# Grouping the logits, softmax and accumulation of the first 20 token tiles in twos

## The chip, the cores and the metric

The kernel runs on one core of one Trainium2 chip. The metric is device time in microseconds (us), the median of repeated executions. One further execution was profiled; all rows below are from it.

## The reference, cut to what matters

Three stages follow one another: attention whose mask lets a query see the keys of its own cluster, a feed-forward layer with the activation h * cos(h), and a soft mixture of experts whose dispatch weights are a softmax over all 3072 tokens. The change touches the second stage and the start of the third.

```
x = attention output, 3072 tokens x 512
h = x @ w_in                                  # 3072 x 2048
g = h * np.cos(h)
x = g @ w_out                                 # 3072 x 512
logits = x @ phi                              # 3072 x 32 slots
d = np.exp(logits - logits.max(0)); d /= d.sum(0) + 1e-09     # over tokens
slot_input = d.T @ x                          # 32 x 512
slot_out = per expert: relu(slot_input @ w1) @ w2
c = np.exp(logits - logits.max(1)); c /= c.sum(1) + 1e-09     # over slots
out = c @ slot_out
```

## The kernel before, in words

Attention takes the first half of the time. Then comes the loop of the feed-forward layer, called the MLP here: 24 tiles of 128 tokens, each in four chunks of 512 hidden columns, so 96 chunks numbered c. For chunk c TensorE computes h (`hchunk`, 12 matmuls of 512 columns into one of three PSUM buffers, `h`). ScalarE and VectorE turn it into g = h * cos(h): a scaled copy on ScalarE and two passes on VectorE (`post1`), then sine, square and a last pass on VectorE that writes `gg` and is the last reader of the PSUM buffer (`post2`; the square is on ScalarE for even chunks and on VectorE for odd ones). TensorE transposes g (`gtr`, tile `gt`), ScalarE copies the transposed chunk to SBUF (`gev`, tile `gts`), and TensorE multiplies it with w_out @ phi, folded beforehand, into the logits of the tile (`logit`, tile `lp`). The product with w_out itself is not formed per token: the kernel accumulates d.T @ g and multiplies that by w_out at the end.

When the four chunks of a tile are through, a running softmax follows over some iterations: `soft1` copies the logits (`lps`), `soft2` sums them up with a constant matrix in both orientations (`lf`, `lt`) and takes the maxima on VectorE (`mrun`, `ng`, `rn`), `softx` and `softe` take the exponentials on ScalarE (`d`, `corr`, `e`), `soft3` updates the sums and writes the normalised weights `ck`, `soft3b` transposes `d` (`dt`, copied to `dts`), `soft4` multiplies it with the tile's g (`accp`) and `soft5` adds that to `acc`. Sine and exponential are in different tables of ScalarE, so each of these softmax steps has two table loads around it.

All instructions stand in the order in which the code writes them, engine by engine; nothing is reordered, and an engine waits at the head of its queue. The loop over c is the order: in iteration c stand `hchunk(c)`, `post2(c-2)`, `post1(c-1)`, `gev(c-4)` and `gtr(c-3)`. So `hchunk(c)` reuses the PSUM buffer that chunk c-3 left, and waits for the `gg` pass of chunk c-3. The softmax steps hang on the last chunk of a tile, by its distance from c: 4 for `soft1`, 5 for `soft2`, 6 for the exponentials, 7 for `soft3` and `soft3b`, 8 for `soft4` and `soft5`. The last two tiles are already one group with an order of their own, and so is the approach to them.

Beside this, the input of the next tile is loaded and split in two parts: `xload` (SyncE's queue, tile `xr`), `xprep` (GpSimd multiply, four VectorE passes, GpSimd add) and `xprep2` (VectorE cast `xhi`, GpSimd subtract `xlo`). `xr` has one buffer, so each `xload` waits in SyncE's queue for the GpSimd subtract before it. The weights of the experts come in 2 MB pieces: four of them go into the pool `wk` of six buffers during the loop (c = 28, 36, 44, 52), the others into buffers of w_in that become free in the last eight chunks, and so on through the tail, in which the DMA engines are busy nearly all the time.

Of the kernel before, what the change touches and what calls it, by code (L numbers as in the profile page):

```python
# [8 lines left out]
F32 = mybir.dt.float32  # L9
# [10 lines left out]
P = 128  # L20
# [6 lines left out]
def clustered_attention_then_soft_moe(  # L27
# [16 lines left out]
    DM, DF = w_in.shape  # L44
# [80 lines left out]
    NC_ = len(order)  # L125
    groups = [[t] for t in range(NT - GRP)] + [list(range(NT - GRP, NT))]
    at_last = {max(c for c in range(NC_) if order[c][0] in ts): ts for ts in groups}
# [637 lines left out]
    with ExitStack() as m:  # L765
# [4 lines left out]
        zero = phis.rearrange("p a s -> p (a s)").bitcast(BF16)  # L770
        POOL.memset(zero, 0.0)
        wo = [wk.tile([P, 8, DM], F32, tag="wk", name=f"wo{x}") for x in range(2)]
        gs_stack = ExitStack()
        gsp = gs_stack.enter_context(tc.tile_pool(name="gsp", bufs=4))

        def post2(c):
            t, f = order[c]
            h, r = R.pop(("h", c)), R.pop(("r", c))
            if f == 0:
                R["g", t] = ggp.tile([P, DF], F32, tag="gg", name=f"gg{t}")  # L780
            ACT.activation(out=r, in_=r, func=AF.Sin, scale=0.5)  # L781
# [14 lines left out]
        def gev(c, eng=None):  # L796
            s = gsp.tile([P, 512], F32, tag="gts", name=f"gts{c}")
            if eng is DVE:
                DVE.tensor_copy(s, R.pop(("gp", c)))
            else:  # L800
                ACT.activation(out=s, in_=R.pop(("gp", c)), func=AF.Copy)
            R["gt", c] = s

        def logit(c):
            t, f = order[c]
            s = R.pop(("gt", c))
            if f == 0:
                if t < NT - GRP:
                    R["lp", t] = psum.tile([P, P], F32, tag="m1", name=f"lp{t}")
# [127 lines left out]
        for c in range(2, NC_):  # L937
# [16 lines left out]
            if c >= 3:  # L954
                gtr(c - 3)
            if c % 4 == 3:
                for x in range(max(c - 7, 0), c - 3):
                    logit(x)
# [9 lines left out]
            if at_last.get(c - 6) == [NT - GRP - 1]:  # L968
                soft3b(at_last[c - 6])
                soft3(at_last[c - 6])  # L970
            elif at_last.get(c - 7) == [NT - GRP - 1]:
                soft4(at_last[c - 7])
            late_c = at_last.get(c - 8)
            if late_c and late_c[0] < NT - GRP - 2:
                soft4(late_c)
                soft5(late_c)
# [4 lines left out]
            if c in (12, 20):  # L981
                x = (c - 12) // 8
                for y in range(2):
                    SP.dma_start(out=wo[x][:, 4 * y:4 * y + 4], in_=wod.rearrange("(f y p) d -> y p f d", f=4, p=P)[2 * x + y])
            if c in (28, 36, 44, 52):
                load_piece((c - 28) // 8, wk, "wk")
            if c == NC_ - 6:
# [256 lines left out]
```

## Time and profile before

| what | value |
|---|---|
| median of 3 runs | 927.43 us (924.83 to 928.53) |
| the profiled execution | 926.85 us, of which the profile's span is 925.1 us |
| TensorE (PE) busy | 884.5 us, 96% of the span |
| VectorE (DVE) busy | 687.6 us, 74% |
| ScalarE (ACT) busy | 668.4 us, 72% |
| GpSimd (POOL) busy | 449.2 us, 49% |
| TensorE's granted clock, mean | 0.986 |

The span reaches from the first instruction to the last. Attention ends and the MLP loop begins at about 470 us, the loop ends at about 857 us. Shares of the span are averages over these stages; what a change in the loop is worth is to be read in the loop.

### The profile page before, as it was taken

How to read it: one execution, taken by the hardware profiler on the slowest of the kernel's cores; microseconds unless marked ns; L12 is line 12 of the kernel's file. 1: busy time of each engine (PE TensorE's matmuls, PEld its weight loads, DVE VectorE, ACT ScalarE, POOL GpSimd, SP SyncE). 2: the span in 40 equal slices, each digit the busy share in tenths (PEclk: the TensorE clock that was granted, in tenths of full speed). 3: DMA queues.
4: the chain of work that ended last, by engine and by line, in shares of the span. 5: the costliest groups of instructions: out<-in, count | busy, mean ns of one | idle time of the engine just before them, and what ended most of it. 6: DMA issues, size and time to landing. Idle time of an engine off the chain costs nothing.

```text
span 925.1 us, 16872 instructions
## 1 busy us (share of the span) xinstructions
PE 884.5 (96%) x6024; PEld 627.5 (68%) x6024; DVE 687.6 (74%) x1459; ACT 668.4 (72%) x1398; POOL 449.2 (49%) x341
## 2 busy tenths in 40 slices
PE   5899999999999999999989999999999999999896
PEld 3576666666667676676557777777777777677443
DVE  6889888888888888988748777777777777776203
ACT  4688888988888898886535777677767777676423
POOL 1477788887777888778442222222222222320000
PEclk8999999999999999999989999999999999999998
DMA  6846656566666656653211322431331010118998
GB/s 160 208 126 169 181 160 175 151 169 163 164 166 176 169 153 165 160 149 101 75 33 47 114 69 92 137 115 39 121 116 45 24 46 23 47 36 325 375 351 301
DMA packets 127790, 129.49 MB, mean 140 GB/s; under 512 B 57838, under 2 KB 105180, under 8 KB 127708
## 3 DMA queue, kind: packets, MB, share of 16 engines
q1 hardware_dynamic: 127708, 128.44, 47.7%
q8 instruction: 47, 0.77, 0.3%
q14 instruction: 35, 0.29, 0.1%
HBM read 86.18 MB, written 16.97 MB: 111 GB/s over the span
## 4 chain that ended last, share of the span: by engine, by line
PE 74%; DVE 8%; ACT 8%; issue 4%; DMA 2%; SPq 2%; POOL 1%; POOLq 0%; ACTq 0%; DVEq 0%
PE h L136 18%; PE o L412 14%; PE sm L362 8%; PE s L399 7%; PE s L400 7%; PE gt L793 3%; PE lp L819 2%; SPq L757 2%; PE accp L902 2%; ACT L781 2%; DVE gg L786 1%; DMA wh<-in_moe_w_dram 1%; PE sum L437 1%; ACT L857 1%; ACT kk L781 1%
## 5 line engine op out<-in xcount | busy, mean ns | idle before, releaser
L136 PE MATMUL h<-wc,xhi 128*128 128x512 f32 x768 | 250.7, 408 | 7.2 <-DVE gg L786 7.1
L364 DVE TENSOR_REDUCE mc<-sm 128x1 f32<-128x384 f32 x384 | 201.2, 552 | 60.9 <-PE sm L362 59.8
L430 POOL TENSOR_TENSOR ps<-ps,a 128x768 f32<-128x768 f32 x120 | 219.7, 1831 | 49.9 <-ACT a L403 45.1
L403 ACT ACTIVATE a<-s 128x384 f32<-128x384 f32 x384 | 179.0, 494 | 28.6 <-PE s L400 25.2
L136 PEld LDWEIGHTS h<-wc,xhi 128*128 128x128 f32 x768 | 138.0, 190 | 57.3 <-DVE kk L145 15.9
L136 PE MATMUL h<-wc,xlo 128*128 128x512 f32 x384 | 152.2, 396 | 0.0
L412 PE MATMUL o<-a,vt 128*64 128x384 f32 x768 | 140.8, 496 | 0.0
L399 PE MATMUL s<-st 96*128 96x384 f32 (+1 forms) x384 | 140.5, 366 | 0.0
L400 PE MATMUL s<-st 128*128 128x384 f32 x384 | 132.0, 344 | 0.0
L362 PE MATMUL sm<-st 96*128 96x384 f32 x384 | 128.0, 374 | 3.0 <-DVE st L335 2.5
L786 DVE SCALAR_TENSOR_TENSOR gg<-kk,h 128x512 f32<-128x512 f32 x96 | 66.0, 688 | 54.9 <-ACT kk L783 51.4
L412 PEld LDWEIGHTS o<-a,vt 128*64 128x64 f32 x768 | 51.0, 136 | 61.2 <-issue 55.6
L362 PEld LDWEIGHTS sm<-st 96*128 96x128 f32 x384 | 71.7, 193 | 30.5 <-issue 9.6
L781 ACT ACTIVATE kk<-kk 128x512 f32<-128x512 f32 x96 | 60.6, 631 | 43.4 <-DVE kk L145 43.0
L107 POOL TENSOR_TENSOR xr<-xr 128x512 f32<-128x512 f32 x24 | 31.7, 1322 | 112.8 <-DMA xr<-recs 102.8
L136 PEld LDWEIGHTS h<-wc,xlo 128*128 128x128 f32 x384 | 72.4, 189 | 17.1
L399 PEld LDWEIGHTS s<-st 96*128 96x128 f32 (+1 forms) x384 | 74.3, 193 | 4.7 <-issue 4.1
L400 PEld LDWEIGHTS s<-st 128*128 128x128 f32 x384 | 73.9, 193 | 0.0
L111 POOL TENSOR_TENSOR xr<-xr 128x512 f32<-128x512 f32 x24 | 31.4, 1307 | 85.5 <-DVE xr L109 81.8
L119 POOL TENSOR_TENSOR xlo<-xr,xhi 128x512 fp32r<-128x512 f32 x24 | 36.5, 1522 | 70.5 <-DVE xhi L118 70.5
L145 DVE SCALAR_TENSOR_TENSOR kk<-kk,h 128x512 f32<-128x512 f32 x96 | 66.0, 688 | 3.3
L427 POOL TENSOR_TENSOR ps<-a,a 128x768 f32<-128x768 f32 x30 | 55.0, 1833 | 22.0 <-ACT a L403 22.0
(216 smaller groups left out, 1501.7 us busy)
## 6 DMA issues: line engine op xcount, KB each, us to landing
st<-st SPq DMA_DIRECT2D x128, 192.0 KB
w<-in_moe_w_dram SPq DMA_DIRECT2D x8, 2048.0 KB
wh<-in_moe_w_dram SPq DMA_DIRECT2D x23, 512.0 KB
w<-in_moe_w_out_dram SPq DMA_DIRECT2D x16, 512.0 KB
w<-in_moe_w_in_dram SPq DMA_DIRECT2D x16, 512.0 KB
qt<-in_q_dram SPq DMA_DIRECT2D x32, 192.0 KB
kt<-in_k_dram SPq DMA_DIRECT2D x32, 192.0 KB
vt<-in_v_dram SPq DMA_DIRECT2D x16, 384.0 KB
```

Of the source, the lines that this page charges most:

```text
L136: PE.matmul(h, lhsT=x[:, d, :], rhs=wc[f][:, w, d, :], start=(n == 0), stop=(n == 3 * DT - 1))
L145: DVE.scalar_tensor_tensor(out=a, in0=a, scalar=-TWO_PI, in1=h, op0=ALU.mult, op1=ALU.add)
L362: PE.matmul(m[:, 0:QW], lhsT=st[0:96, Q1 + h, qt * P:(qt + 1) * P], rhs=st[0:96, K1 + h, half * QW:(half + 1) * QW], start=True, stop=True)
L364: DVE.tensor_reduce(out=s["mc"][:, col:col + 1], in_=m[:, 0:QW], op=ALU.max, axis=AX.X)
L399: PE.matmul(x[:, 0:QW], lhsT=st[0:n, K1 + h, ks], rhs=st[0:n, Q1 + h, qs], start=True, stop=False)
L400: PE.matmul(x[:, 0:QW], lhsT=st[:, K2 + h, ks], rhs=st[:, Q2 + h, qs], start=False, stop=True)
L403: ACT.activation(out=T[i][u][:, h, :], in_=x[:, 0:QW], func=AF.Exp, scale=scale)
L412: PE.matmul(s["o"][64 * h:64 * h + 64, 0:QW], lhsT=s["v"][:, h, kt, :], rhs=t[:, h, :], start=(kt == 0), stop=(kt == KT - 1))
L427: (DVE if i == NPAIR - 1 else POOL).tensor_tensor(out=ps, in0=s[u - 1], in1=t, op=ALU.add)
L430: (DVE if i == NPAIR - 1 else POOL).tensor_tensor(out=ps, in0=ps, in1=t, op=ALU.add)
L781: ACT.activation(out=r, in_=r, func=AF.Sin, scale=0.5)
L786: DVE.scalar_tensor_tensor(out=R["g", t][:, f * 512:(f + 1) * 512], in0=r, scalar=0.5, in1=h, op0=ALU.subtract, op1=ALU.mult)
```

## The change

The first 20 tiles form ten groups of two, `NPR = 20`; tiles 20 and 21 stay alone and the last two stay as they were. A pair's logits are computed in one piece once per eight chunks, into one PSUM tile of two halves, and all softmax steps are done once for 256 tokens. `soft4` and `soft5` of a pair come 12 chunks after its last chunk in place of 8 (for the pair 18 and 19 they stay at 8). What must live longer gets room: eight slots for the transposed chunks (`gtx`) and two more buffers for g (`gx`) take two of the six buffers of `wk`. The weight pieces 2 and 3, which would have had these buffers, are loaded at c = 84 and 88 in place of 44 and 52. The functions `soft1` to `soft5` are not edited; they were written for a group of any size.

```diff
@@ -123,7 +123,8 @@
     order = [(t, f) for t in range(NT - GRP) for f in range(NF)]
     order += [(t, f) for f in range(NF) for t in range(NT - GRP, NT)]
     NC_ = len(order)
-    groups = [[t] for t in range(NT - GRP)] + [list(range(NT - GRP, NT))]
+    NPR = 20
+    groups = [[t, t + 1] for t in range(0, NPR, 2)] + [[t] for t in range(NPR, NT - GRP)] + [list(range(NT - GRP, NT))]
     at_last = {max(c for c in range(NC_) if order[c][0] in ts): ts for ts in groups}
 
     def hchunk(c):
@@ -769,6 +770,8 @@
         R["m"] = m0
         zero = phis.rearrange("p a s -> p (a s)").bitcast(BF16)
         POOL.memset(zero, 0.0)
+        gtx = wk.tile([P, 8, 512], F32, tag="wk", name="gtx")
+        gx = wk.tile([P, 2, DF], F32, tag="wk", name="gx")
         wo = [wk.tile([P, 8, DM], F32, tag="wk", name=f"wo{x}") for x in range(2)]
         gs_stack = ExitStack()
         gsp = gs_stack.enter_context(tc.tile_pool(name="gsp", bufs=4))
@@ -777,7 +780,10 @@
             t, f = order[c]
             h, r = R.pop(("h", c)), R.pop(("r", c))
             if f == 0:
-                R["g", t] = ggp.tile([P, DF], F32, tag="gg", name=f"gg{t}")
+                if t < NPR and t % 5 > 2:
+                    R["g", t] = gx[:, t % 5 - 3]
+                else:
+                    R["g", t] = ggp.tile([P, DF], F32, tag="gg", name=f"gg{t}")
             ACT.activation(out=r, in_=r, func=AF.Sin, scale=0.5)
             if c == NC_ - 2 or (c % 4 in (0, 2)):
                 ACT.activation(out=r, in_=r, func=AF.Square)
@@ -794,7 +800,7 @@
             R["gp", c] = g
 
         def gev(c, eng=None):
-            s = gsp.tile([P, 512], F32, tag="gts", name=f"gts{c}")
+            s = gtx[:, c % 8] if c < NF * NPR else gsp.tile([P, 512], F32, tag="gts", name=f"gts{c}")
             if eng is DVE:
                 DVE.tensor_copy(s, R.pop(("gp", c)))
             else:
@@ -805,7 +811,11 @@
             t, f = order[c]
             s = R.pop(("gt", c))
             if f == 0:
-                if t < NT - GRP:
+                if t < NPR:
+                    if t % 2 == 0:
+                        R["lpg"] = psum.tile([P, 2, P], F32, tag="m1", name=f"lp{t}")
+                    R["lp", t] = R["lpg"][:, t % 2, :]
+                elif t < NT - GRP:
                     R["lp", t] = psum.tile([P, P], F32, tag="m1", name=f"lp{t}")
                 elif t == NT - GRP:
                     R["lpg"] = psum.tile([P, GRP, P], F32, tag="m1", name="lpg")
@@ -953,8 +963,12 @@
                 soft3b(late_c)
             if c >= 3:
                 gtr(c - 3)
-            if c % 4 == 3:
-                for x in range(max(c - 7, 0), c - 3):
+            if c < NF * (NPR + 1):
+                if c % 8 == 3:
+                    for x in range(max(c - 11, 0), c - 3):
+                        logit(x)
+            elif c % 4 == 3:
+                for x in range(c - 7, c - 3):
                     logit(x)
             if c - 4 in at_last:
                 soft1(at_last[c - 4])
@@ -970,8 +984,12 @@
                 soft3(at_last[c - 6])
             elif at_last.get(c - 7) == [NT - GRP - 1]:
                 soft4(at_last[c - 7])
+            late_c = at_last.get(c - 12)
+            if late_c and late_c[0] < NPR - 2:
+                soft4(late_c)
+                soft5(late_c)
             late_c = at_last.get(c - 8)
-            if late_c and late_c[0] < NT - GRP - 2:
+            if late_c and NPR - 2 <= late_c[0] < NT - GRP - 2:
                 soft4(late_c)
                 soft5(late_c)
             if c == 5:
@@ -982,8 +1000,8 @@
                 x = (c - 12) // 8
                 for y in range(2):
                     SP.dma_start(out=wo[x][:, 4 * y:4 * y + 4], in_=wod.rearrange("(f y p) d -> y p f d", f=4, p=P)[2 * x + y])
-            if c in (28, 36, 44, 52):
-                load_piece((c - 28) // 8, wk, "wk")
+            if c in (28, 36, 84, 88):
+                load_piece((28, 36, 84, 88).index(c), wk, "wk")
             if c == NC_ - 6:
                 w8 = R["mxa"].tile([P, 1024], F32, tag="xr", name="w8b", bufs=1)
                 load_part(8, 2, w8)
```

The order of instructions shows this at three places. Names carry the tile's or chunk's number and a buffer number; the lines of the changed kernel stand up to ten lower than before.

TensorE before, at the end of chunk 47: the transposes of chunk 44 are followed by the logits of tile 10 and the accumulation of tile 9.

```order
L136 MATMUL h47_8191<-wc3_97,xlo11_8002 128x512
L793 MATMUL gt44_8217<-ident_68,gg11_8164 128x128 x4
L819 MATMUL lp10_8222<-gts40_8090,wphi_79 32x128 x4
L819 MATMUL lp10_8222<-gts41_8130,wphi_79 32x128 x4
L819 MATMUL lp10_8222<-gts42_8172,wphi_79 32x128 x4
L819 MATMUL lp10_8222<-gts43_8211,wphi_79 32x128 x4
L902 MATMUL accp9_8241<-gg9_7812,dts9_8189 32x512 x4
L136 MATMUL h48_8247<-wc0_94,xhi12_8178 128x512 x2
```

TensorE with the change, at the same chunk: between h47 and h48 stand the transposes alone.

```order
L137 MATMUL h47_8000<-wc3_97,xlo11_7797 128x512
L137 MATMUL h47_8000<-wc3_97,xhi11_7796 128x512 x2
L137 MATMUL h47_8000<-wc3_97,xlo11_7797 128x512
L799 MATMUL gt44_8025<-ident_68,gg11_7972 128x128 x4
L137 MATMUL h48_8030<-wc0_94,xhi12_7986 128x512 x2
```

TensorE with the change, four chunks later, at the end of chunk 51: the logits of tiles 10 and 11 in one piece (one row for all of the eight chunks' slots) and the accumulation of the pair 8 and 9.

```order
L137 MATMUL h51_8119<-wc3_97,xlo12_7987 128x512
L799 MATMUL gt48_8144<-ident_68,gg12_8101 128x128 x4
L829 MATMUL lp10_8149<-gtx_6283,wphi_79 32x128 x32
L912 MATMUL accp8_8184<-gx_6284,dts8_7998 32x512 x8
L137 MATMUL h52_8194<-wc0_94,xhi13_8110 128x512 x2
```

So what stood behind every fourth chunk now stands twice as long behind every eighth. ScalarE before, around the exponentials of tile 9 (kk44 is the sine argument of chunk 44, in L781 the sine itself, in L783 its square):

```order
L143 ACTIVATE kk44_8126<-h44_8070 128x512
L801 ACTIVATE gts41_8130<-gt41_8092 128x512
L857 ACT_TABLE_LOAD
L857 ACTIVATE d9_8135,ds9_8133<-lf9_8097,ng9_8101 128x128
L858 ACTIVATE corr9_8132<-mrun8_7925,ng9_8101 128x1
L865 ACTIVATE e9_8136,es9_8134<-lf9_8097,rn9_8102 128x32
L781 ACT_TABLE_LOAD
L781 ACTIVATE kk44_8126<-kk44_8126 128x512
L783 ACTIVATE kk44_8126<-kk44_8126 128x512
L143 ACTIVATE kk45_8168<-h45_8110 128x512
```

ScalarE with the change, around the exponentials of the pair 8 and 9, at the same chunk:

```order
L807 ACTIVATE gtx_6283<-gt41_7901 128x512
L867 ACT_TABLE_LOAD
L867 ACTIVATE d8_7942,ds8_7940<-lf8_7906,ng8_7911 128x256
L868 ACTIVATE corr8_7939<-mrun6_7595,ng8_7911 128x1
L875 ACTIVATE e8_7943,es8_7941<-lf8_7906,rn8_7912 128x32 x2
L787 ACT_TABLE_LOAD
L787 ACTIVATE kk44_7934<-kk44_7934 128x512
L789 ACTIVATE kk44_7934<-kk44_7934 128x512
L144 ACTIVATE kk45_7976<-h45_7918 128x512
```

The block is the same but for `d` of 256 columns and two exponentials `e`; it stood four chunks later once more before, and now does not. SyncE's queue before, where weight pieces 2 and 3 stand among the loads of tiles 11 to 15 (behind the load of tile 23 comes piece 4 there):

```order
L98 DMA xr11_7861<-xnum1_82 128x4x128
L101 DMA xr11_7861<-recs1_90 64x4x128 x2
L98 DMA xr12_8036<-xnum2_83 128x4x128
L101 DMA xr12_8036<-recs2_91 64x4x128 x2
L762 DMA w2_8108<-in_moe2_w1_dram 128x4x1024
L98 DMA xr13_8213<-xnum2_83 128x4x128
L101 DMA xr13_8213<-recs2_91 64x4x128 x2
L98 DMA xr14_8388<-xnum2_83 128x4x128
L101 DMA xr14_8388<-recs2_91 64x4x128 x2
L762 DMA w3_8460<-in_moe2_w1_dram 128x4x1024
L98 DMA xr15_8565<-xnum2_83 128x4x128
L101 DMA xr15_8565<-recs2_91 64x4x128 x2
```

SyncE's queue with the change, from the load of tile 23 on:

```order
L98 DMA xr22_9339<-xnum3_84 128x4x128
L101 DMA xr22_9339<-recs3_92 64x4x128 x2
L98 DMA xr23_9478<-xnum3_84 128x4x128
L101 DMA xr23_9478<-recs3_92 64x4x128 x2
L763 DMA w2_9499<-in_moe2_w1_dram 128x4x1024
L763 DMA w3_9679<-in_moe2_w1_dram 128x4x1024
L763 DMA w4_9716<-in_moe2_w1_dram 128x4x1024
```

Both pieces now stand directly behind the last tile's load and ahead of piece 4.

## Rows read from the trace of the kernel before

**Rows 1.** Chain that ended last: logits behind chunks 11 and 75 (start us, us, line).

```profile
518.07 1.01 PE lp L819 x32
...
771.51 1.01 PE lp L819 x32
```

**Rows 2.** Waits of TensorE, 430 to 900 us (total us, times, longest us).

```profile
PE h L136 <- DVE gg L786: 7.1, 11, 1.6
```

**Rows 3.** Timeline of PE, chunks 40 to 44 (start us, us, line, op, out<-in, count).

```profile
630.84 0.73 PE L136 MATMUL h<-wc,xhi 128*128 128x512 f32 x2
...
634.18 0.39 PE L835 MATMUL lf<-lps,gmat 128*128 128x128 f32 x2
...
634.54 0.71 PE L136 MATMUL h<-wc,xhi 128*128 128x512 f32 x2
...
641.07 0.27 PE L890 MATMUL dt<-ident,d 128*128 128x128 f32 x1
641.18 0.74 PE L136 MATMUL h<-wc,xhi 128*128 128x512 f32 x2
...
644.62 1.08 PE L819 MATMUL lp<-gts,wphi 128*32 128x128 f32 x32
...
646.49 0.72 PE L136 MATMUL h<-wc,xhi 128*128 128x512 f32 x2
```

**Rows 4.** Timeline of ACT in the same stretch: a softmax step between its table loads.

```profile
635.60 1.28 ACT L857 ACT_TABLE_LOAD   x1 [0.51 <-DVE rn L844]
636.89 0.37 ACT L857 ACTIVATE d<-lf,ng 128x128 f32<-128x128 f32 x1
...
637.43 0.28 ACT L865 ACTIVATE e<-lf,rn 128x32 f32<-128x32 f32 x1
...
637.82 1.28 ACT L781 ACT_TABLE_LOAD   x1
```

**Rows 5.** Timeline of DVE in the same stretch.

```profile
634.75 0.29 DVE L841 TENSOR_REDUCE mrun<-lf 128x1 f32<-128x128 f32 x1 [1.35 <-PE lf L837]
...
640.44 0.69 DVE L786 SCALAR_TENSOR_TENSOR gg<-kk,h 128x512 f32<-128x512 f32 x1 [1.56 <-ACT kk L783]
...
642.62 0.24 DVE L883 TENSOR_SCALAR ck<-e,es 128x32 f32<-128x32 f32 x1
642.77 0.42 DVE L118 CAST xhi<-xr 128x512 fp32r<-128x512 f32 x1
...
643.82 0.69 DVE L786 SCALAR_TENSOR_TENSOR gg<-kk,h 128x512 f32<-128x512 f32 x1
644.43 0.79 DVE L144 TENSOR_SCALAR kk<-kk 128x512 f32<-128x512 f32 x1
```

**Rows 6.** Page, costliest groups: a VectorE reduce of 384 columns (mean ns).

```profile
L364 DVE TENSOR_REDUCE mc<-sm 128x1 f32<-128x384 f32 x384 | 201.2, 552 | 60.9 <-PE sm L362 59.8
```

**Rows 7.** Timeline of DVE and of POOL, two tiles earlier.

```profile
602.99 0.87 DVE L842 TENSOR_TENSOR mrun<-mrun,mrun 128x1 f32<-128x1 f32 x1
...
602.54 1.30 POOL L107 TENSOR_TENSOR xr<-xr 128x512 f32<-128x512 f32 x1 [5.34 <-DMA xr<-recs]
```

**Rows 8.** Line 785, chunk loop from 500 us (duration ns min/median/max).

```profile
L785 DVE TENSOR_TENSOR kk<-kk x42: 680/683/1627, 499.7 to 828.2; 128x512 f32<-128x512 f32 x42
```

**Rows 9.** Timelines of SP and POOL: two tile loads and the multiplies that wait for them.

```profile
629.31 0.37 SPq L98 DMA_DIRECT2D xr<-xnum  x1
...
644.96 0.37 SPq L98 DMA_DIRECT2D xr<-xnum  x1
...
646.64 0.61 SPq L762 DMA_DIRECT2D w<-in_moe_w_dram  x1
...
633.60 1.28 POOL L107 TENSOR_TENSOR xr<-xr 128x512 f32<-128x512 f32 x1 [4.32 <-DMA xr<-recs]
...
649.81 1.28 POOL L107 TENSOR_TENSOR xr<-xr 128x512 f32<-128x512 f32 x1 [4.88 <-DMA xr<-recs]
```

**Rows 10.** PE at chunk 87; piece 4's issue; a window (ends: clock, DMA share, GB/s).

```profile
822.43 1.04 PE L902 MATMUL accp<-gg,dts 128*32 128x512 f32 x8
...
830.17 0.38 SPq L762 DMA_DIRECT2D w<-in_moe_w_dram  x1
...
648.00:652.00 4.00, 4.00 (x23) 3.37 (x22) 2.52 (x8) 2.40 (x5) 1.28 (x1) 1.00 0.99 321
```

## The prediction

> **What bounds the kernel now.** I read the busy table first: TensorE is busy nearly all the time, the other engines about three quarters. In the chunk loop, then, only two things can move the end: work that TensorE itself does, and time in which TensorE waits. So the chain that ended last comes next. From the logits behind chunk 11 to those behind chunk 75, 16 tiles, it takes 771.51 - 518.07 = 253.44 us [rows 1], 15.84 us a tile. The timeline of TensorE gives what a tile costs without any wait: from the start of h40 (630.84) to the start of h44 (646.49) it is 15.65 us [rows 3]. The difference, 0.19 us a tile or 0.38 us a pair, is waiting. The table of waits says on whom: h waits for the `gg` pass of VectorE, 7.1 us over the loop in 11 waits, the longest 1.6 us [rows 2]. That pass reads the PSUM buffer that h wants. All that ScalarE and VectorE save is worth at most what stands in that row.
>
> When does `gg` come late? The timelines of the three engines around one softmax step tell it [rows 3 to 5]. The sums `lf` stand on TensorE from 634.18 to the next h at 634.54. VectorE starts on their maxima at 634.75. ScalarE begins the first table load at 635.60, after 0.51 us of waiting for `rn`, then the exponentials, and at 637.82 the load back. Sine and square follow, and only then `gg` of chunk 40, at 640.44 to 641.13. TensorE starts h43, which wants its buffer, at 641.18, directly behind the transpose `dt` (641.07). In this tile TensorE arrives 0.05 us after `gg`, so any delay of a softmax step beyond 0.05 us is a wait. Behind h43 stand logits and accumulation, from 644.62 to 646.49, 1.87 us in which ScalarE and VectorE catch up.
>
> **What goes.** Of two softmax steps in eight chunks one goes, and with it two table loads of 1.28 us [rows 4]; over ten pairs 20 loads, 25.6 us of ScalarE. They cost the end only where `gg` is late, which is counted above as 0.38 us a pair.
>
> TensorE loses little. One `lf` block takes 0.36 us [rows 3]; that of a pair has twice the columns and two small products, so between 0.36 and 0.72, where two single blocks took 0.72. Most of it streams columns, I take 0.61, a gain of 0.1. From h43 to the logits it was 3.44 us, from h40 to the `lf` block 3.34 [rows 3]: the way into the logits costs 0.1 more, and goes once a pair. For the double block of logits and accumulation I take between 3.74 and 3.6, a gain of up to 0.1. Together 0.3 us a pair, between 0.1 and 0.4.
>
> **What is added.** I walk the tile of rows 3 to 5 again, as a pair; its h40 to h44 are h44 to h48 in the changed order. The `lf` block is 0.25 longer. The reduce over 256 columns takes 0.13 more: 0.29 us for 128 columns [rows 5], 0.552 for 384 [rows 6]. `rn` has 64 columns, some hundredths more. So the first table load starts 0.4 later. `d` over 256 columns costs between nothing and another 0.37 [rows 4]; since the reduce grew by less than half when its width doubled, I take 0.1. The second `e` costs 0.39 (637.43 to 637.82). Together `gg` is 0.9 later. TensorE itself comes to h47 later by 0.25 and by a second `dt` of 0.11. The wait there is 0.9 - 0.36 - 0.05 = 0.5 us, where two waits of 0.19 on average stood.
>
> It does not end there, as the logits and the accumulation no longer stand behind h47. TensorE needs 3.34 us for a chunk with its transposes. From `gg` to the next `gg` it was 3.38 us (640.44 to 643.82) [rows 5], and the second `ck` adds 0.15 (642.62 to 642.77), so h48 waits another 0.2. The next round: `gg` 0.61 to the pass L144, which is held at 0.79 us in this place [rows 5], a pass of 0.69, and 1.34 for sine and square (637.82 + 1.28 to 640.44), with the hand-overs 3.5 us; h49 waits 0.15 to 0.2. The rounds after it have neither `ck` nor a held pass, and the 3.7 us behind h51 absorb what is left. New waits: 0.9 us a pair, between 0.5 (if h48 and h49 have slack) and 1.3.
>
> Per pair that makes -0.3 - 0.38 + 0.9 = +0.2 us, for ten pairs +2 us.
>
> The first tile has a softmax step of its own while the loop starts, and that becomes part of the first pair; the longest wait of rows 2 is 1.6 us, and I take 1 us less, between 0 and 1.6.
>
> **Where VectorE and GpSimd meet.** In one tile `mrun` on VectorE took 0.87 us, and its end, 603.86, is the end of GpSimd's multiply (602.54 + 1.30) [rows 7]. The multiply of odd chunks on VectorE, 0.683 us in the median, took 1.627 once [rows 8]. So these two-input passes stand still while GpSimd works. In the changed order `xhi` of the pair's second tile comes at about 643.8 (642.77 + 0.9 + 0.15), and the GpSimd multiply 2.19 us for the subtract (642.77 to the load at 644.96) and 4.29 to 4.85 us for the load later [rows 5, 9], at 650.3 to 650.9. The multiply of chunk 47 is ready after `gg` of chunk 45 (643.82 + 1.05), 3.5 us to that of chunk 46, 0.61, a pass like the cast's 0.42 and one of 0.69 to the sine, and half of the 1.34 for the sine itself: 650.8. Who is first changes from pair to pair. If GpSimd is, VectorE loses 0.94 us, of which h50 has some 0.2 in hand: 0.75 us. I count two such pairs, +1.5 us.
>
> The Trainium skill, "SBUF — State Buffer", section "Who interferes with whom", has it that VectorE with two SBUF inputs and a GpSimd instruction that reads SBUF exclude each other, and that the one that issues first has the port for its whole instruction. The end of `mrun` at the end of GpSimd's multiply agrees with it, and by that rule a pair in which GpSimd is first loses all of GpSimd's remaining time.
>
> **The late weights.** Piece 3 needs `gx`, which the accumulation at chunk 87 frees at 823.47 (822.43 + 1.04); piece 4 starts at 830.17 [rows 10]. In these 6.7 us a piece of 2.1 MB passes at 321 GB/s in 6.5. It just fits, and I take nothing; begun only with piece 4, it would cost its 6.5 us in a tail that the DMA engines fill. Piece 2 is earlier by four chunks and stands behind the load of tile 23. With a piece directly behind it a load took 4.85 us to its multiply, without one 4.29 [rows 9]: 0.6 us at most, once, taken as nothing.
>
> **Sum.** Against the profiled execution's 926.85 us, which is 0.6 below the median of 927.43 and inside its range: 926.85 + 2 - 1 + 1.5 = 929.4, so 929 us.
>
> **The rivals.** *The waits vanish (faster).* If ScalarE's step starts earlier than walked, say because no GpSimd pass meets `mrun` any more (by the walk GpSimd's first multiply is over before the pair's `lf`), the 0.5 at h47 shrinks, and with it those of h48 and h49, which only follow. It decides if `gg` comes 0.5 us sooner than walked. Then a pair gains 0.3 + 0.38, ten pairs 6.8 us, and with the first tile's 1 us the time is 919; with half of the waits gone, 922. For it speaks that VectorE and ScalarE have less to do per pair; against it, that one step is one chain, and it got longer. Chance 0.28.
>
> The Trainium skill, "ScalarE: Activation LUTs", sections "What ACT_TABLE_LOAD costs" and "Table sets: the hidden batching unit", says to batch activations by table set, and puts a switch at 2.66 us with its drain, 53 us for the 20 that go. In this trace `d` starts 1.29 us after the load does, so half of that is seen here. By the rule the time would come out as this rival's 919, since more than the waits can't be regained.
>
> *GpSimd is first in most pairs (slower).* Place: the multiply of chunk 47. Price 0.75 us a pair, 7.5 in ten: 926.85 + 2 - 1 + 7.5 = 935. It decides if the load's latency is below about 4.8 us in most pairs; of the two in rows 9 one is below and one above. Chance 0.22.
>
> *The late weights cost (slower).* Piece 3 overlaps piece 4 and the tail shifts: up to 6.5 us more on the sum, 932 to 936. Chance 0.05.
>
> *Nothing comes of it.* TensorE's 0.3 us a pair is all that changes, the waits stay in sum: 924. Chance 0.05.
>
> **How the numbers follow.** The forecast has 0.40; its own range, from waits of 0.5 to 1.3 a pair, is 925 to 933. The bounds of no difference, 0.5% of 927.43, about what a measurement here can tell, are 922.8 and 932.1. Faster holds nearly all of the first rival, 0.27. Slower holds most of the second, of the third, and the forecast's upper edge, 0.27. The rest, 0.46, is the same. The range goes from 921, half of the first rival, to 935.
>
> **What would show it.** ScalarE's exponential blocks drop from 23 to 13. The lf block is 0.6 us, and `d` at 256 columns about 0.47. TensorE waits for `gg` about 0.5 us at h47 and every eighth h before and behind it, and about 0.2 at the two that follow each of them. The logits and accumulation stand in one piece of some 3.7 us. The multiply of chunk 47 and its like is long where GpSimd's multiply overlaps it. Piece 3 lands before piece 4 starts, and the tail from 860 us on keeps its shape. The prediction is wrong if h47 starts without a wait, if a chain of waits runs on to h51, or if the loop's end moves otherwise than its waits do.

## The result, and the profile after

| | before | after |
|---|---|---|
| median of 10 runs | 926.49 us (923.64 to 929.08) | 933.34 us (930.73 to 935.69) |
| ratio, 95% interval | | 1.0076 [1.0056, 1.0096] |
| the profiled execution | 926.85 us, span 925.1 | 930.73 us, span 929.0 |

The change makes the kernel slower by 0.76%, about 7 us. The time lies in the prediction's whole range (921 to 935), above its likeliest value of 929 and just above the forecast's own 925 to 933. The two profiled executions are only 3.9 us apart: that of before is 0.4 above its median, that of after is the fastest of its ten. Further runs of both kernels (first experiment) put them about 6 us apart.

The busy line of the page comes first, that of the changed kernel.

```profile
PE 885.5 (95%) x6004; PEld 626.9 (67%) x6004; DVE 679.2 (73%) x1369; ACT 634.0 (68%) x1328; POOL 446.7 (48%) x341
```

ScalarE has lost 34 us of work (668.4 before) and VectorE 8 (687.6). TensorE has as much as before. So two engines were relieved, and the kernel got slower. Next the waits of TensorE from 430 to 900 us (total us, times, longest us); `gg` of two tiles in five now has the name `gx`.

```profile
PE h L137 <- DVE gg L792: 4.8, 12, 1.0
PE h L137 <- DVE gx L792: 4.5, 8, 1.4
```

Together 9.3 us in 20 waits, where it was 7.1 in 11 [rows 2]. The chain that ended last (start us, us, line) shows logits and accumulation in one piece.

```profile
514.63 1.93 PE lp L829 x64
...
545.96 1.89 PE lp L829 x64
547.85 1.72 PE accp L912 x16
...
578.52 1.89 PE lp L829 x64
...
611.00 1.88 PE lp L829 x64
...
643.49 1.88 PE lp L829 x64
```

A pair takes 32.5 us from piece to piece (643.49 - 611.00), where two tiles of before took 31.68 [rows 1: 253.44 us for 16 tiles]. What lies between is best seen as the time from the start of one h to that of the next, worked out from TensorE's timeline of each kernel. The pattern repeats every eight chunks: what the prediction says of h44 to h51 is seen below at h36 to h43, with h39 in the place of h47, h40 of h48, h41 of h49, h42 of h50.

```
us from   h36   h37   h38   h39   h40   h41   h42   h43   h36 to h44
before   3.70  3.22  3.51  5.30  3.70  3.22  3.42  5.30   31.38
after    4.13  3.24  3.95  3.54  3.48  3.90  3.26  6.99   32.49
```

The next eight chunks of after, h44 to h52, differ from these in one place: 3.24 in place of 3.90, then 3.42 in place of 3.26, 32.01 in sum. The timeline of TensorE in the stretch h36 to h44 of after (start us, us, what; in brackets the wait ahead):

```profile
614.53 0.73 PE L137 MATMUL h<-wc,xhi 128*128 128x512 f32 x2
...
617.86 0.60 PE L845 MATMUL lf<-lps,gmat 128*128 128x256 f32 x2
...
618.66 0.71 PE L137 MATMUL h<-wc,xhi 128*128 128x512 f32 x2
...
625.22 0.38 PE L900 MATMUL dt<-ident,d 128*128 128x128 f32 x2
...
625.85 0.72 PE L137 MATMUL h<-wc,xhi 128*128 128x512 f32 x2 [0.25 <-DVE gx L792]
...
629.39 0.73 PE L137 MATMUL h<-wc,xhi 128*128 128x512 f32 x2
...
636.77 0.73 PE L137 MATMUL h<-wc,xhi 128*128 128x512 f32 x2 [0.41 <-DVE gx L792]
...
643.42 1.95 PE L829 MATMUL lp<-gtx,wphi 128*32 128x128 f32 x64
```

The h at 625.85 and that at 636.77 wait. The gaps that TensorE shows as idle (0.25 and 0.41) are smaller than the delays, since the matmuls' ends are modelled; the starts are the better measure. VectorE in the same stretch, and the like of its multiply in the next eight chunks (667.05):

```profile
618.86 0.43 DVE L851 TENSOR_REDUCE mrun<-lf 128x1 f32<-128x256 f32 x1 [1.79 <-PE lf L847]
619.32 0.16 DVE L852 TENSOR_TENSOR mrun<-mrun,mrun 128x1 f32<-128x1 f32 x1
...
625.11 0.69 DVE L792 SCALAR_TENSOR_TENSOR gx<-kk,h 128x512 f32<-128x512 f32 x1 [1.94 <-ACT kk L789]
...
628.65 0.69 DVE L792 SCALAR_TENSOR_TENSOR gx<-kk,h 128x512 f32<-128x512 f32 x1
629.25 0.79 DVE L145 TENSOR_SCALAR kk<-kk 128x512 f32<-128x512 f32 x1
...
632.13 0.69 DVE L792 SCALAR_TENSOR_TENSOR gx<-kk,h 128x512 f32<-128x512 f32 x1 [1.36 <-ACT kk L789]
...
634.57 1.42 DVE L791 TENSOR_TENSOR kk<-kk 128x512 f32<-128x512 f32 x1 [0.70 <-ACT kk L787]
636.03 0.69 DVE L792 SCALAR_TENSOR_TENSOR gx<-kk,h 128x512 f32<-128x512 f32 x1
...
667.05 0.69 DVE L791 TENSOR_TENSOR kk<-kk 128x512 f32<-128x512 f32 x1 [0.70 <-ACT kk L787]
...
668.38 0.79 DVE L145 TENSOR_SCALAR kk<-kk 128x512 f32<-128x512 f32 x1
```

Each late h starts directly behind a `gx` pass: 625.11 + 0.69 gives 625.80 and h39 at 625.85, 628.65 + 0.69 gives 629.34 and h40 at 629.39, 632.13 + 0.69 gives 632.82 and h41 at 632.87. `mrun` is short (0.16). The multiply of chunk 39 at 634.57 takes 1.42 us in place of 0.69, and `gx` behind it ends at 636.72, h42 starts at 636.77. GpSimd says why (its timeline, one load later too):

```profile
634.15 1.30 POOL L107 TENSOR_TENSOR xr<-xr 128x512 f32<-128x512 f32 x1 [4.39 <-DMA xr<-recs]
...
667.57 1.32 POOL L107 TENSOR_TENSOR xr<-xr 128x512 f32<-128x512 f32 x1 [5.33 <-DMA xr<-recs]
```

And SyncE's queue, the loads which these two multiplies wait for, and later the late weights:

```profile
629.79 0.36 SPq L98 DMA_DIRECT2D xr<-xnum  x1
...
662.26 0.37 SPq L98 DMA_DIRECT2D xr<-xnum  x1
...
816.01 18.51 SPq L763 DMA_DIRECT2D w<-in_moe_w_dram  x3
```

At 634.15 GpSimd was first and VectorE, ready at 634.57, stood until GpSimd's end at 635.45 and ended 0.54 later. At 667.05 VectorE was first by half a microsecond and this multiply lost nothing; but the one-input pass behind it (668.38) took 0.79 us in place of 0.42 beside GpSimd's multiply, and the next h is late by 0.2 (the 3.42 above). Both loads were issued 15.25 us behind the start of their eight chunks (629.79 - 614.53, 662.26 - 647.02), and VectorE was ready 20.03 behind it both times (634.57 and 667.05); the load took 4.36 us to the multiply in the first and 5.31 in the second. In the nine stretches from chunk 12 to 84 this load took 4.34 to 4.52 us seven times and 5.3 twice. In six of the seven VectorE's multiply was held; in the seventh (h76 to h84) it came 1.7 us later than usual, behind passes that waited for the input of a tile.

ScalarE's timeline in the softmax step:

```profile
612.95 0.38 ACT L836 ACTIVATE lps<-lp 128x256 f32<-128x256 f32 x1 [2.81 <-PE lp L829]
...
619.88 1.28 ACT L867 ACT_TABLE_LOAD   x1 [1.11 <-DVE rn L854]
621.17 0.47 ACT L867 ACTIVATE d<-lf,ng 128x256 f32<-128x256 f32 x1
...
622.48 1.28 ACT L787 ACT_TABLE_LOAD   x1
623.77 0.64 ACT L787 ACTIVATE kk<-kk 128x512 f32<-128x512 f32 x1
```

The table load waits 1.11 us for `rn`, though it has no operand: the load carries the wait of the exponential behind it. Before, that wait was 0.51 in the step shown [rows 4]. The whole-kernel account, from starts of h: h12 to h84 takes 293.5 us after and 287.3 before (+6.2); h4 to h12 takes 28.61 and 31.39 (-2.8), since logits, softmax and accumulation of the first tile are put off; h84 to h92 takes 33.61 and 32.53 (+1.1), where put-off work is done; and h2 starts 0.6 us earlier. From h95 to the end both have 74.0 us. The sum is +3.9, the profiled difference. The edit does not reach what stands ahead of h2: over the thirteen profiles of this document h2 starts between 479.6 and 482.2 us, so the 0.6 is scatter, and the change itself makes +4.5 in these two profiles.

### The profile page after: what moved, and what is told of

Same layout as the page of the kernel before. It is cut to its first block, busy times and chain, and to the rows that moved or that the text cites. A ratio compares the mean times of both kernels' runs of the same rounds, so it can differ in the third digit from the quotient of the medians.

```text
span 929.0 us, 16674 instructions
## 1 busy us (share of the span) xinstructions
PE 885.5 (95%) x6004; PEld 626.9 (67%) x6004; DVE 679.2 (73%) x1369; ACT 634.0 (68%) x1328; POOL 446.7 (48%) x341
## 4 chain that ended last, share of the span: by engine, by line
PE 66%; DVE 14%; ACT 9%; issue 4%; DMA 2%; SPq 2%; POOL 1%; POOLq 0%; ACTq 0%; DVEq 0%
PE o L413 14%; PE h L137 12%; PE sm L363 8%; PE s L400 7%; PE s L401 7%; DVE kk L146 2%; ACT kk L787 2%; PE lp L829 2%; DVE kk L791 2%; DVE gg L792 2%; PE gt L799 2%; SPq L758 2%; PE accp L912 2%; DMA wh<-in_moe_w_dram 2%; ACT L787 2%
## 5 line engine op out<-in xcount | busy, mean ns | idle before, releaser
L792 DVE SCALAR_TENSOR_TENSOR gg<-kk,h 128x512 f32<-128x512 f32 x64 | 43.9, 687 | 45.7 <-ACT kk L789 42.8
L400 PEld LDWEIGHTS s<-st 96*128 96x128 f32 (+1 forms) x384 | 73.9, 192 | 4.4 <-issue 3.4
L119 POOL TENSOR_TENSOR xlo<-xr,xhi 128x512 fp32r<-128x512 f32 x24 | 33.8, 1408 | 60.2 <-DVE xhi L118 60.2
```

Of the source, the lines that this page charges most:

```text
L400: PE.matmul(x[:, 0:QW], lhsT=st[0:n, K1 + h, ks], rhs=st[0:n, Q1 + h, qs], start=True, stop=False)
L792: DVE.scalar_tensor_tensor(out=R["g", t][:, f * 512:(f + 1) * 512], in0=r, scalar=0.5, in1=h, op0=ALU.subtract, op1=ALU.mult)
```

## The experiments

Two theories stood against each other. Theory A: the loss stands in the pattern of eight chunks. One softmax step of a pair is a longer chain than one of a tile and makes h47 late; logits and accumulation, which covered that before, stand elsewhere, so h48 and h49 are late too; and VectorE's multiply meets GpSimd's. Rival B: the weight pieces that are loaded late cost it. All ratios are to the kernel before, run on the same chip beside the experiment. The experiments are numbered e0 to e10, as their expectations name them.

**The changed kernel again (e0).**

> The changed kernel once more, to see how far one profile of it stands for its other runs. Theory A (the time is lost in the eight-chunk cycle: a wait of about 0.45 us at h47, 0.2 at h48 and h49 each because logits and accumulation no longer stand behind h47, and 0.65 at h50 in each pair in which GpSimd's multiply is ahead of VectorE's): ratio to the kernel before 1.005 to 1.009, and in six or more of the nine cycles from chunk 12 a multiply of 1.4 us or more ahead of the late h50; the cycles with it take 32.5 us and those without it 32.0. Rival B (the late weight pieces lose it in the tail): the same ratio, but the tail from the last logits to the end is over 2 us longer than before.

931.66 us, 1.0056 [1.0035, 1.0077]. The stretches of eight chunks are the same to some hundredths (32.48 to 32.59 with the held multiply, but for the first with 33.15, and 32.01 without), GpSimd is first in the same six, and the tail is as long (73.9 us). So neither the collision nor its place is chance.

**The accumulation back at 8 chunks** (e1), all else as in the change:

```diff
-            late_c = at_last.get(c - 12)
-            if late_c and late_c[0] < NPR - 2:
-                soft4(late_c)
-                soft5(late_c)
             late_c = at_last.get(c - 8)
-            if late_c and NPR - 2 <= late_c[0] < NT - GRP - 2:
+            if late_c and late_c[0] < NT - GRP - 2:
```

> The changed kernel with the accumulation of every pair 8 chunks after its last chunk, behind h47 as before, in place of 12. Theory A: its 1.7 us behind h47 cover what h48 to h50 waited for; the intervals h47 to h48 and after it hold no wait, a cycle takes 31.3 to 31.6 us in place of 32.5, and the time falls by 7 to 9 us against the changed kernel, to a ratio of 0.997 to 1.001 to the kernel before. The wait at h47 of 0.45 us stays. Rival B: nothing changes, ratio 1.005 to 1.009. Rival C (the double block of logits and accumulation itself stalls TensorE): the block is half as long, and the cycle gets shorter by less than 0.3 us.

924.22 us, 0.9979 [0.9961, 0.9998], 7.4 us less than the changed kernel on the same chip. TensorE, ScalarE and VectorE do the same work, but the accumulation of a pair now stands behind h47 and the logits behind h51. Its chain:

```profile
578.82 1.88 PE lp L829 x64
...
610.37 1.88 PE lp L829 x64
```

31.55 us a pair. The intervals, h36 to h44, are 4.12, 3.22, 3.96, 5.29, 3.24, 3.24, 3.23, 5.29. The wait at h47 is there as in the changed kernel (3.96), but h48 and h49 are on time, and the late multiply at h50 costs nothing, although it is still held in most stretches (1.41 us at 600.66): the 1.9 us of accumulation let VectorE and ScalarE catch up, as the logits and the accumulation did in the kernel before. So the order alone cost all that the changed kernel lost. A third theory of the expectation, that the double block of logits and accumulation itself stalls TensorE, falls with e9 below, which keeps the block and loses nothing.

**The late weights alone** (e2), on the kernel before:

```diff
-            if c in (28, 36, 44, 52):
-                load_piece((c - 28) // 8, wk, "wk")
+            if c in (28, 36, 84, 88):
+                load_piece((28, 36, 84, 88).index(c), wk, "wk")
```

> The kernel before with nothing changed but the time at which weight pieces 2 and 3 are loaded, chunks 84 and 88 in place of 44 and 52. Theory A: no difference, ratio 0.998 to 1.002. Rival B: 3 to 7 us slower, ratio 1.003 to 1.008, with the tail longer by that.

926.87 us, 1.0005 [0.9992, 1.0019]: no difference that the runs tell. In its one profile the stretch from h95 to the end takes 75.5 us in place of 74.0, but over the thirteen profiles this stretch takes from 73.9 to 76.0, and in the changed kernel it takes 74.0 and 73.9. Rival B falls.

One thing this kernel can't show: here both buffers are free from the start, while in the changed kernel piece 3 waits for `gx`. There SyncE's queue (a wait: total us, times, longest us; then start us, us) and the windows (us, then busy us of PE, PEld, DVE, ACT and POOL with their instructions, clock, DMA share, GB/s) tell how it fits:

```profile
SPq L763 <- PE accp L912: 10.9, 1, 10.9
...
827.52 7.00 SPq L763 DMA_DIRECT2D w<-in_moe_w_dram  x2
...
834.15 0.37 SPq L763 DMA_DIRECT2D w<-in_moe_w_dram  x1
```

```profile
820.00:824.00 4.00, 3.72 (x20) 2.91 (x19) 3.39 (x13) 3.32 (x7) 0.46 (x1) 1.00 0.90 366
824.00:828.00 4.00, 4.00 (x57) 2.22 (x56) 3.35 (x6) 1.60 (x4) 2.51 (x2) 1.00 0.00 0
828.00:832.00 4.00, 4.00 (x23) 3.38 (x22) 2.54 (x8) 2.58 (x5) 0.39 (x1) 1.00 0.88 295
```

Between 824 and 828 us the DMA engines stand still: piece 2 is over, and piece 3 waits for the accumulation that reads `gx`. It is issued at 827.52 and piece 4 at 834.15, 6.6 us later, in which a piece just passes.

**The square of every eighth chunk on ScalarE** (e3), in the changed kernel, so that VectorE has no two-input multiply where GpSimd's stands:

```diff
-            if c == NC_ - 2 or (c % 4 in (0, 2)):
+            if c == NC_ - 2 or (c % 4 in (0, 2)) or (c % 8 == 7 and c < NF * NPR):
```

> The changed kernel with one square per pair moved from VectorE to ScalarE, that of chunks 15, 23, ... 79 (chunk 47 and its like), so that GpSimd can't hold it. Theory A: the 0.65 us at h50 goes in the six or seven cycles that had it, every cycle takes 32.0 us, and the time falls by 3.5 to 5 us against the changed kernel; the waits at h47 to h49 stay. Rival B: nothing changes. A rival within A, that GpSimd's overlap is only beside the late h50 and ScalarE's order is what delays it: the cycle stays at 32.5 us.

927.07 us, 1.0010 [0.9997, 1.0022], 4.6 us less than the changed kernel. The interval from h41 to h42 and its like is 3.24 to 3.26 in eight of the nine stretches (the ninth waits for a load there), and seven of them take 31.80 to 31.87 us. The waits at h47, h48 and h49 stay (3.95, 3.54, 3.48). So with this multiply away from VectorE the six stretches gain about 0.67 each (32.5 to 31.83), a little more than the expectation's 32.0 a stretch. The two in which VectorE came first gain 0.18 as well, since the interval behind h50 is 3.23 to 3.25 in place of 3.42.

**The table of exponentials loaded early** (e4), with the accumulation at 8. A one-column exponential that waits for nothing is issued ahead of `softx`, so that the load in front of it no longer waits for `rn`:

```diff
+                ACT.activation(out=ones[:, 1:2], in_=ones[:, 0:1], func=AF.Exp)
```

> The accumulation at 8 as in e1, and ahead of each softmax step one exponential of a single column that waits for nothing, so that the table load goes before the wait for the maxima and not behind it. Theory A: the load of 1.28 us then runs beside the 1.1 us in which ScalarE waited, the exponentials start about 0.95 us sooner, and the wait of 0.45 us at h47, the last one in the cycle, goes. Interval h46 to h47 3.5 us in place of 3.96, cycle 31.1 us in place of 31.55; 3 to 5 us less than e1, ratio to the kernel before 0.992 to 0.996. A rival, that h47 waits for TensorE's own transposes of d and not for the chain through ScalarE: h47 stays at 3.96 and the ratio at 0.998.

924.05 us, 0.9981 [0.9966, 0.9996], in the profile 31.45 us a pair in place of 31.55: the forecast gain did not come. ScalarE's timeline tells why:

```profile
645.38 0.38 ACT L836 ACTIVATE lps<-lp 128x256 f32<-128x256 f32 x1 [3.65 <-PE lp L829]
...
650.38 1.28 ACT L955 ACT_TABLE_LOAD   x1
```

And in e1, without the early line:

```profile
649.11 1.28 ACT L867 ACT_TABLE_LOAD   x1 [0.22 <-DVE rn L854]
```

The forecast took the wait of 1.1 us from the changed kernel; in e1 the load waited only 0.22. Half of that pays for the extra exponential (the next ACTIVATE starts 0.11 behind it, as in e7 below), and 0.1 is left: h46 to h47 takes 3.86 in place of 3.96. Where the logits have no accumulation behind them, `lps` stands later against the next h (here it starts 0.13 us behind h44, in the changed kernel 1.58 ahead of h36: 612.95 against 614.53), and ScalarE comes to the load later by its own work. In the kernel before and in the changed one the accumulation gives ScalarE a lead, which it then spends waiting for `rn`. The rival of this expectation, TensorE's transposes of `d`, falls with e7, which has the same transposes and 3.45.

**The logits every four chunks** (e5), in the changed kernel:

```diff
-            if c < NF * (NPR + 1):
-                if c % 8 == 3:
-                    for x in range(max(c - 11, 0), c - 3):
-                        logit(x)
-            elif c % 4 == 3:
-                for x in range(c - 7, c - 3):
+            if c % 4 == 3:
+                for x in range(max(c - 7, 0), c - 3):
                     logit(x)
```

> The changed kernel, accumulation at 12 as it was, but with the logits of a pair in two blocks of four chunks, so that one block of 0.9 us stands behind h47. Theory A (any work behind h47 covers the waits, whichever it is): 0.9 us cover the 0.2 of h48 and the 0.2 of h49 and most of the 0.65 at h50; cycle 31.5 to 31.7 us in place of 32.0 and 32.5, 6 to 8 us less than the changed kernel, ratio 0.998 to 1.001. If it is the accumulation's place alone that matters: cycle 32.0 to 32.5, ratio 1.005 to 1.008.

925.58 us, 0.9988 [0.9974, 1.0001]. Intervals 4.14, 3.24, 3.94, 4.43, 3.25, 3.23, 3.21, 6.13, sum 31.57. Here half of the logits stands behind h47, and 1.1 us of it do nearly as well as the 1.9 of the accumulation: with the held multiply the interval up to h50 or its like is 3.23 in four stretches and 3.29 to 3.43 in three. It matters that something stands there, not what.

**The early table load alone, on the kernel before** (e6 and e10; the line of e4, run twice, on two chips).

> The kernel before with the same early exponential ahead of every softmax step. Theory A: the waits of 0 to 0.9 us at h43 and its like (the load behind a maximum that GpSimd held) go; most cycles take 31.3 us, 2 to 5 us less, ratio 0.995 to 0.998. If those waits have another cause: ratio 1.000.

> The kernel before with the early exponential, once more, on the chip of these two. Theory A: cycle 31.1 us, ratio 0.993 to 0.997, the same as the pairs with their waits taken away.

922.40 us, 0.9954 [0.9935, 0.9973], and 921.16 us, 0.9945 [0.9928, 0.9962]. The chain of the second:

```profile
533.86 1.01 PE lp L819 x32
549.41 1.01 PE lp L819 x32
564.96 1.01 PE lp L819 x32
```

15.55 us a tile without a wait, 31.09 a pair, where it was 31.68. By the ratios one line gives 4 to 5 us: the wait of the load for `rn` was what made `gg` late. What varied it was GpSimd's hold on `mrun` [rows 7]: in the kernel before the interval up to h15 is 3.41 where `mrun` took 0.16 us, and the one up to h55 is 3.91 where it took 0.67. In e10 `mrun` is held as before (0.70 and 0.75 us between h28 and h36), and the interval is 3.34 every time.

**The early table load in the changed kernel (e7).**

> The changed kernel as it is (accumulation at 12) with the early exponential. Theory A: gg of chunk 44 comes 0.95 us sooner, the wait at h47 goes and 0.5 us of slack stand there, which the longer rounds at h48 and h49 use up; at h50 up to 0.6 us of wait stay where GpSimd's multiply is first. Cycle 31.0 to 31.6 us, 7 to 10 us less than the changed kernel, ratio 0.995 to 0.999. Rival (h48 to h50 wait for lack of cover whatever h47 does): only the 0.45 goes, cycle 31.6 to 32.1, ratio 1.001 to 1.004.

925.95 us, 0.9997 [0.9978, 1.0016], 5.7 us less than e0 on another chip: less than the 7 to 10 forecast, with a ratio between those of theory A and of its rival. ScalarE's timeline of it:

```profile
648.28 1.28 ACT L955 ACT_TABLE_LOAD   x1
649.57 0.20 ACT L955 ACTIVATE ones<-ones 128x1 f32<-128x1 f32 x1
649.68 0.46 ACT L867 ACTIVATE d<-lf,ng 128x256 f32<-128x256 f32 x1
```

The load waits for nothing, `d` follows at once. In h36 to h44 the intervals are 4.13, 3.22, 3.45, 3.24, 3.29, 4.00, 3.24, 6.99: the three waits of the chain are gone in most stretches, and the collision at h50 stands as before. This takes the chain's part and the collision's part apart.

**Logits every four chunks and the early load together (e8).**

> The pairs with the logits in blocks of four (e5) and the early exponential (e4, e6): ScalarE keeps its lead from the accumulation behind the logits, and something stands behind h47. Theory A (TensorE's own work is the floor, and it is the same for pairs and single tiles): no wait is left, the cycle takes 31.1 us as in e6, ratio to the kernel before 0.993 to 0.997. Rival (the fewer table loads and passes are worth something of their own): cycle below 30.8 us, ratio below 0.992. If the early exponential again does nothing for pairs, as in e4: cycle 31.6, ratio 0.999.

921.09 us, 0.9947 [0.9933, 0.9962]; undisturbed stretches take 31.04 to 31.07 us, others up to 31.5, and the last, which waits for a load, 32.6.

**The changed kernel with both cures** (e9), the early load and the square on ScalarE.

> The changed kernel (logits and accumulation of a pair behind h51) with the early exponential (e7) and the square of chunks 15, 23, ... 79 on ScalarE (e3), that is with both causes of theory A taken away and nothing else moved. Theory A: cycle 30.9 to 31.2 us, ratio 0.993 to 0.997. If a third cause is left in the double block or in the room it takes: cycle over 31.4, ratio over 0.998.

920.52 us, 0.9936 [0.9916, 0.9956], the lowest median of all; its interval overlaps those of the two kernels above with the early load. Its chain:

```profile
577.74 1.88 PE lp L829 x64
...
608.55 1.88 PE lp L829 x64
...
639.37 1.88 PE lp L829 x64
```

30.81 us a pair. Against the 31.09 of the kernel before with the early load this is what the grouping itself is worth: 0.28 us a pair. Five of the nine stretches take 30.80 to 30.82; three still have waits (31.62, 31.86 and 31.45), and the last waits for a load, as in all kernels. Of the three the first has no accumulation ahead of it, so that ScalarE comes late as in e4. In the other two GpSimd's first multiply meets VectorE's one-input pass; in h44 to h52 (VectorE, then GpSimd):

```profile
644.30 1.41 DVE L145 TENSOR_SCALAR kk<-kk 128x512 f32<-128x512 f32 x1
...
644.13 1.29 POOL L107 TENSOR_TENSOR xr<-xr 128x512 f32<-128x512 f32 x1 [5.58 <-DMA xr<-recs]
```

The pass takes 0.42 us alone. ScalarE's sine behind it, and with it the table load, comes 0.9 us later than in the stretch before, and h46 to h47 takes 3.90 in place of 3.45. In the changed kernel the same pass was held for 1.22 us in the same stretch and the interval stayed at 3.96: there the load had to wait for `rn` anyway. The early load takes away that wait, and with it the room in which this collision was hidden; e7 and e8 have such stretches too (the pass at 1.07 to 1.49 us, h46 to h47 or its like at 3.53 to 3.97).

## Why the prediction was nearly right, and where it was not

The mechanism held, and one term of the sum was mis-sized most: the step "I count two such pairs, +1.5 us". The forecast was +2.5 us, the medians differ by 6 to 7: 933.3 lies above the 932.1 that the prediction set as its bound of no difference, so the kernel is slower by that bound, to which it gave 0.27, and "the same" had 0.46. By its points:

- **TensorE bounds the loop, and only waits for `gg` count.** Shown. ScalarE lost 34 us of work and the time rose.
- **TensorE's own work, -0.3 a pair.** 0.28, by the last experiment against the kernel before with the early load. Its parts were off and made up for each other: the `lf` block is 0.80 us (617.86 to 618.66), not 0.61, and the piece of logits and accumulation is 3.60 (643.42 to 647.02), the lower end of the bounds. That they came to the sum forecast is luck.
- **The waits that go, 0.38 a pair.** They were 0.59: with the early load the kernel before takes 31.09 a pair, and 31.68 without. The stretch taken as free of waits, 15.65 us from h40 to h44, had 0.1 of them itself; a tile without any takes 15.55.
- **The wait at h47, 0.5 us.** h46 to h47 is 3.95, and 3.45 with the early load, in which the second `dt` is already contained: 0.50.
- **h48 0.2, h49 0.15 to 0.2.** The intervals up to them are 3.54 and 3.48 against 3.24 where no wait is left: 0.30 and 0.24. The walk had the rounds right (3.38 + 0.15 and 3.5 us) and TensorE's chunk wrong: the 3.34 that it set against them is the way from h40 to the `lf` block, a plain chunk takes 3.22 to 3.24. That the missing cover is the reason is shown by the two kernels that put work behind h47. With the wait at h47 and 0.16 behind h50 the new waits are 1.2 a pair (32.01 - 30.81), against 0.9 forecast. The 0.16 is a wait of h51 and its like, small, but at the h that the prediction named in a sign of being wrong (a chain of waits that runs on to h51); it comes from the held pass at 668.38, in a place that the walk took as free.
- **Net +0.2 a pair without collisions.** The undisturbed stretches take 32.01, the mean of before from h12 to h76 is 31.68: +0.33, which is -0.28 - 0.59 + 1.20. The errors of the two terms of waits nearly cancel.
- **The collision.** The threshold was right: the prediction put it at a latency below 4.8 us, and the trace puts it at 4.78 (20.03 - 15.25). The share of pairs was not. In seven of nine the load took less, in six of these the multiply was held, and the same six do it in the second profiled run. Two loads were shown to judge it by [rows 9]; the trace of before had more, and of its 21 tile loads behind 500 us 12 took less than 4.8 us to their multiply. The price is 0.7 at h50, of which 0.16 comes back at h51, so 0.5 net (32.49 against 32.01), or 0.67 against the kernel without that multiply, and not 0.75. Six by 0.5 to 0.67 is 3 to 4 us, where 1.5 stood. So the forecast and its rival "GpSimd is first in most pairs" both hold in part: the rival's "most" came true, at a somewhat lower price and on fewer pairs than its ten. The Trainium skill, "SBUF — State Buffer", section "Who interferes with whom", says that the one that issues first has the shared port for its whole instruction. The two multiplies above agree: the one that came 0.42 us behind GpSimd's start took 1.42 us, the one that came 0.52 ahead took 0.69.
- **The first tile, -1 us.** -2.8 in chunks 4 to 12, of which 1.1 is paid back in chunks 84 to 92, so -1.7, just beyond the 1.6 allowed; the forecast did not follow the put-off work to its end.
- **The late weights, nothing.** Shown by the kernel that has them alone, and by the changed kernel's end, as long as before; there the 6.7 us worked out between `gx` and piece 4 were 6.6.
- **The rival in which the waits vanish.** Its reason came true: `mrun`, held up to 0.87 us in the softmax steps of before up to chunk 76, took 0.16 in all of the changed kernel. Its condition, `gg` 0.5 us sooner, was not met by the change, but by the early load. With both cures the kernel stands at 920.5, near the 919 worked out for that rival. The Trainium skill, "ScalarE: Activation LUTs", section "Table sets: the hidden batching unit", says to batch by set; here 20 loads less, 25.6 us of ScalarE, went with a slower kernel, as ScalarE did not bound it.

In the profiles, then: eight stretches of +0.33 or so, six collisions of 0.5, some 0.6 in the first stretch (there the one-input pass is held for 1.27 us), and -1.7 before and behind them, about +4.5; the 0.6 us ahead of h2 come off that. What stays open is the difference of the medians, 6 to 7 us. Part of it lies in which execution was profiled (the lowest of ten). In the ten runs the time goes roughly with the mean granted clock, from 931.1 us at 0.991 to 935.6 at 0.980 (but 934.05 at 0.988), and the profiled one had 0.987; the runs of before in e0 spread over the same clocks. The start of h2 and the stretch from h95 on each scatter by more than 2 us over the profiles, so single profiles can't place the remaining 2 us.

## What to carry to other kernels

Work that stands behind a possibly late instruction in an in-order queue is its cover; before moving work, ask which wait it hid, since the same work four chunks earlier was worth 7 us here. Relieving an engine that doesn't bound the kernel buys nothing by itself, and merging two short serial steps into one longer one can cost, as the wait depends on the longest chain and not on the mean. When two events race for a port, compare their times to a common start in several periods: a threshold inside the spread of a load's latency makes a collision in most periods, or in few, and the count is the term to bound, from every load that the trace has.

## What the hardware showed that was not expected

A table load on ScalarE takes up the wait of the activation behind it: 15.4 us in 19 waits between 500 and 830 us for `rn` before, 7.6 in 9 after. A one-column exponential ahead (0.20 us) parts the two, and is worth 4 to 5 us in the kernel before by the ratios, and 0.1 us a pair where the wait was 0.22.

The two-input multiply on VectorE that was held by GpSimd took between 1.40 and 1.63 us in place of 0.69; `TENSOR_SCALAR`, with one input tile, took 0.79 in place of 0.42 (629.25) beside the subtract of GpSimd and up to 1.41 beside its multiply (644.30 in e9). The pass with one input in PSUM and one in SBUF took 0.68 to 0.69 in all rows of the changed kernel's loop.

The load of a tile of input, from its issue to the multiply that uses it, took 4.34 to 4.52 us in seven of the nine places that decide the collision in the changed kernel and 5.3 in two, none of them with a weight piece behind it. The same two places (the stretches from h44 and from h68) are the long ones in e0 (5.09 and 4.95; the others 4.32 to 4.48). What makes the difference was not tried.
